# Second pair's B and C loaded in 2,048-byte pieces and turned by TensorE, first pair's loads first on two queues, seven filler matmuls

## The chip, the cores and the metric

The kernel runs on one core of a Trainium2 chip. The metric is the device time of one execution in microseconds (us); lower is better. A core has TensorE (PE; its weight loads are listed as PEld), VectorE (DVE), ScalarE (ACT), GpSimd (POOL) and SyncE (SP), each with an instruction queue of its own that is worked off in order. SP, and in the change ACT too, issue DMAs; all of them share 16 DMA engines. TensorE writes to PSUM banks, the other engines read those.

## What is computed

Two stages, cut to what matters here. The first is a scan over 768 positions for 4 x 8 (batch, head) pairs, in chunks; the second is a gated feed-forward layer on its result.

```python
# x: (4, 8, 768, 32), a: (4, 8, 768), B and C: (4, 8, 768, 16), all f32
cum = np.cumsum(log(clip(a, 1e-6, 1)) of the chunk)
L = np.exp(cum_i - cum_j), causal
y_intra = ((C @ B.T) * L) @ x
y_inter = (C @ state) * exp(cum)
y = y_intra + y_inter
state = exp(sum) * state + sum_j B_j x_j exp(cum_end - cum_j)
...
xf = y as (4 * 768, 256)
gate = 1 / (1 + np.exp(-(xf @ w_gate)))          # w_gate, w_val: (256, 1536)
out = (gate * (xf @ w_val)) @ w_out              # w_out: (1536, 256)
```

## The kernel before

The 768 positions are cut into six chunks of 128 (two halves of 64, the inner step of the scan). A *unit* is one chunk of one batch element with its eight heads; two units make a pair. For the first chunk (class `FirstUnit`) the pairs are laid out otherwise: unit u = 2 * late + k holds the *half* `late` of the chunk, and each half of the 128 partitions is another batch element. So the first pair (units 0 and 1, late = 0) is the first 64 positions of all four batch elements, and the second pair (units 2 and 3, late = 1) the other 64. Only the second pair needs a state from before it.

For a unit of the first chunk the steps are:

- `load_first`: SP loads B, C (tiles `bn`, `cn`) and x (`xn`) of a pair, two DMAs for each (line 274). For B and C the innermost contiguous run is 16 numbers, 64 bytes; for x it is 32 numbers, 128 bytes.
- `spread` (line 572): TensorE spreads the decays `apart` over partitions into `pa` (line 580), DVE scans them (line 586) into `ab`.
- `products` (line 377): TensorE transposes B and C (lines 386, 387) into `pt`, ACT copies the result to `bct`, B once and C masked for two groups (lines 397 to 401), and TensorE multiplies the two in `multiply` (line 464) into `pcb`.
- `decayed` (line 425): B times the decay at the end (`bd`, line 429, on DVE or POOL).
- `first_results` (line 604): DVE weighs the products by the decays (`weigh`, line 478, result `m`), TensorE multiplies by x (`within`, lines 490 and 497). The second pair adds the part from the state (line 624).
- `first_outputs` (line 629): ACT copies the output to `xw` (line 636); `first_states` makes the state from the rest.

The feed-forward layer takes the 1,536 hidden columns in 12 blocks f of 128. A weight tile holds two blocks of one matrix, so tiles w0 (gate) and w1 (value) serve blocks 0 and 1, w2 and w3 serve blocks 2 and 3, and so on to w11; w12 to w17 are `w_out`. Each is loaded with one DMA of 512 KB (lines 304 and 308, in runs of 2,048 and 1,024 bytes) and converted by `split_w` (DVE line 318, ACT 323, DVE 325, ACT 329, POOL 331); some are then cut into a high and a low part (`part_w`, lines 346 and 348). In the first chunk, blocks 0 to 5 use the converted weights as they are: blocks 0 to 3 in two halves, `half_gate` and `half_value` (line 714, 256 columns; half i takes the units of pair i), blocks 4 and 5 whole (line 804). From block 6 on, and in all later chunks, high and low parts are multiplied in three combinations (line 813). `proj` multiplies by `w_out` (lines 839, 850, 851) and stores the result.

TensorE starts with `WARM = 3` matmuls on zeros (line 126).

The order of the instructions in the engines' queues is set when the program is built, by a planner (`run`, line 180). Every piece of work is a task, a generator that yields steps; a step names its engine, an estimated cost, the keys it needs and the keys it makes. The planner keeps an estimated time for each engine, takes the step that could begin first, and among those of the same engine that could begin within `HOLD` of it the one with the earliest due time. `DUES` overrides the due times of single tasks; the load order at the start comes from `FIRST` with due times from -100 on. What the planner estimates sets only the order; on the chip, semaphores make an instruction wait for what it needs. SP issues all loads and stores in its planned order.

PSUM has three banks of the tag `mm` (used in turn by `pa`, the gates and values, `po`), one bank `py` (`warm`, `pt`) and four banks `pcb`.

Of the kernel before, what the change touches and what calls it, by code (L numbers as in the profile page):

```python
# [17 lines left out]
DUES = {  # L18
# [13 lines left out]
}  # L32
WARM = 3


FIRST = "b0 c0 w0 x0 w1 b1 c1 w2 x1 w3 r w4 w5 w6 w7 w8 w9"
LANES = 8
# [22 lines left out]
STATE = 30.0  # L60
SPARE = 1.0


# [4 lines left out]
def tile_ssd_then_gated_ffn(  # L68
# [111 lines left out]
    def run():  # L180

        free = {"sp": 1.0, "pe": 1.2 + 1.7 * WARM, "act": 3.5, "dve": 6.0, "pool": 6.2, "none": 0.0}
        port_free = [0.0]
        dma_free = 0.0
        landed = [0.0] * LANES

        turns, turn_of = [0.0] * 3, {}
        made = {}
        spare = {"y": [0.0], "banks": [0.0] * 3, "cb": [0.0], "g": [0.0] * 3, "o": [0.0] * 2}
        tasks.sort(key=lambda t: t[:2])  # L190
        while tasks:
# [78 lines left out]

    def load_first(tag, src, late, n):
        t = pair_of(tag, 0, 2 * late, n)
        for i in range(2):
            nc.sync.dma_start(  # L274
                t[i * L2 : (i + 1) * L2].rearrange("p u h n -> p (u h) n"),
                src[late * L2 : (late + 1) * L2, 2 * i * H : 2 * (i + 1) * H],
            )

    def load_a(c, b):
# [89 lines left out]
    class Unit:  # L369
# [7 lines left out]
        def products(self):  # L377

            c, b, u = self.c, self.b, self.u
            needs = [("bc", u)] if c else [("bc", u), ("b0", u // 2)]  # L380
            if c:
                needs += [("bct", u - 1 if c > 1 else -1), ("cb", u - 4), ("cd", u - 4)]
            yield step("pe", 0.24 if c else 0.45, needs, [("tp", u)], y=1)
            bn, cn = (got[k, c, b // 2][:, b % 2].rearrange("p h n -> p (h n)") for k in ("bn", "cn"))
            pt = ps_y.tile([P, 512], F32, tag="py", name=f"pt{self.nm}")
            nc.tensor.transpose(pt[:, :L], bn, eye)  # L386
            nc.tensor.transpose(pt[:, L : 2 * L], cn, eye)
            yield step("act", 0.9 if c else 1.1, [], [("bct", u)], y=-1)
            if c:
                self.bct = wk.tile([P, 4, L], F32, tag="bct", name=f"bct{self.nm}", bufs=4)  # L390
            else:

                if ("bct", b // 2) not in got:
                    got["bct", b // 2] = hp.tile([P, 2, 4, L], F32, tag=f"h{5 + b // 2}", name=f"bct{self.nm}")
                self.bct = got["bct", b // 2][:, b % 2]
            if u > 1:
                nc.scalar.copy(self.bct[:, :2].rearrange("p k l -> p (k l)"), pt[:, : 2 * L])
            else:
                nc.scalar.copy(self.bct[:, 0], pt[:, :L])
# [3 lines left out]
            if c == 0:  # L403
                yield step("pe", 0.47, [("cb", u - 1)] if u % 2 else [], [("cb", u)], **({} if u % 2 else {"cb": 1}))
                if u % 2 == 0:
                    got["pcb"] = ps_cb.tile([P, NQ, 512], F32, tag="pcb", name=f"pcb{self.nm}")
                multiply(got["pcb"], u % 2, self)
            elif u == NB + 1:
# [160 lines left out]
    class FirstUnit(Unit):  # L569


        def spread(self):

            u = self.u
            yield step("pe", 1.0, [("a0",)], banks=1)
            pa = ps_mm.tile([P, 512], F32, tag="mm", name=f"pa{u}")
            rows = slice(32 * (u // 2), 32 * (u // 2) + 32)
            for i in range(2):
                b = 2 * i + u % 2
                nc.tensor.matmul(  # L580
                    pa[i * L2 : (i + 1) * L2], of_b2[rows, b : b + 1].broadcast_to([32, L2]),
                    apart[rows].rearrange("p h l -> p (h l)"), start=True, stop=True,
                )
            yield step("dve", 1.22, [], [("scan", u)], banks=-1)
            self.dec = ld.tile([P, H, L2], F32, tag="ab", name=f"ab{self.nm}", bufs=NDEC)
            nc.vector.tensor_tensor_scan(
                out=self.dec.rearrange("p h l -> p (h l)"), data0=pa, data1=delta.rearrange("p h l -> p (h l)"),
                initial=0.0, op0=ALU.mult, op1=ALU.add,
            )
# [11 lines left out]
        def decays(self):  # L601
            yield from self.decayed()

    def first_results(*two):
# [24 lines left out]
    def first_outputs(late):  # L629

        for i in range(2):
            yield step("act", ACT_HALF, [("inter" if late else "y", 2 * late + 1)], [("xf", late)] if i else [])
# [3 lines left out]
            nc.scalar.copy(out, got["py", late][:, i, :, 0])  # L636

# [307 lines left out]
    def initial():  # L945
# [6 lines left out]
        yield step("none", 0.0, [], made)  # L952
        yield step("none", 4.9, [], [("a0",)])

    task(-60.0, "", initial())
# [7 lines left out]
    for late in range(2):  # L963
        for tag, src, n, needs, makes in (
            ("b", b4, N, [], [("b0", late)]),
            ("c", c4, N, [], [("bc", 2 * late), ("bc", 2 * late + 1)]),
            ("x", x4, D, [], [("xn", 2 * late), ("xn", 2 * late + 1)]),
        ):
            loads[f"{tag}{late}"] = load(
                2, 1.9 if tag == "x" else 1.5, needs, makes, lambda a=(f"{tag}n", src, late, n): load_first(*a)  # L970
            )
    for i in range(NW):
# [8 lines left out]
    def unit(due, c, b):  # L981
# [9 lines left out]
        if c or b > 1:  # L991
            task(due, f"before{u.nm}", u.before())
        task(due - (0.0 if c else 30.0), f"products{u.nm}", u.products())
        task(due, f"decays{u.nm}", u.decays())
        if c == 0 and b % 2:
            task(due, f"result{u.nm}", first_results(pair.pop(), u))
            task(due, f"outputs{u.nm}", first_outputs(b // 2))
# [71 lines left out]
```

## Time and profile before

| | us |
|---|---|
| median of 3 runs | 373.65 (373.58 to 373.71) |
| profiled execution | 374.85, its span 373.0 |
| TensorE busy in the span | 360.9 |
| mean granted TensorE clock | 0.982 of full |
| HBM read / written | 22.41 MB / 3.34 MB |

The span runs from the first to the last instruction that the profile records; the time of a run holds a little more. A line of the order of time has the start, the time taken, the engine, the line of the kernel, the operation, what it writes and reads, how many such instructions, and, in brackets, how long the engine had been idle before and what ended that. A matmul on f32 data appears as two PE instructions. "issue" means that the profile shows nothing that the engine waited for.

### The profile page before, as it was taken

Reading aid. Unit: us, or ns where it says so; the run is one execution under the profiler, and the core shown is the slowest. Engines: PE = TensorE matmul, PEld = TensorE weight load, DVE = VectorE, ACT = ScalarE, POOL = GpSimd, SP = SyncE. Lnnn points to the kernel's source line nnn. Section 1 sums busy time; section 2 is a strip of 40 time slices with the busy share of each in tenths; the row PEclk is TensorE's granted clock in tenths of the full one; section 3 lists DMA queues with packets and bytes.
Section 4 is the critical chain, followed back from the end, with each engine's and each line's share of the span. In section 5 each row is a group of like instructions: output and inputs, shape, how many; then the busy total and the mean of one; then the engine's idle time right before and its main releaser. Section 6 shows DMA issues by size and latency. Waiting matters only on the chain.

```text
span 373.0 us, 8123 instructions
## 1 busy us (share of the span) xinstructions
PE 360.9 (97%) x3376; PEld 287.0 (77%) x3376; DVE 157.0 (42%) x277; ACT 151.1 (41%) x314; POOL 150.1 (40%) x159
## 2 busy tenths in 40 slices
PE   7788999999999999999999999999999999999996
PEld 2267668877878888888878888788877788888885
DVE  4756557768435444553354622430224440222201
ACT  2656686423575411544511245430254420254400
POOL 4425476463797520244440045430144420145410
PEclk9669999999999999999999999999999999999999
DMA  6999996527236322502332300400000000000000
GB/s 121 208 233 184 243 314 169 96 44 122 67 30 113 30 71 60 106 22 34 26 99 82 89 4 6 53 10 29 30 1 2 2 2 28 30 0 0 2 28 28
DMA packets 89270, 26.27 MB, mean 70 GB/s; under 512 B 76306, under 2 KB 82002, under 8 KB 89234
## 3 DMA queue, kind: packets, MB, share of 16 engines
q1 hardware_dynamic: 89234, 25.76, 31.8%
q8 instruction: 26, 0.43, 0.5%
q14 instruction: 10, 0.08, 0.1%
HBM read 22.41 MB, written 3.34 MB: 69 GB/s over the span
## 4 chain that ended last, share of the span: by engine, by line
PE 88%; SPq 5%; DMA 4%; POOL 1%; issue 1%; DVE 0%; ACT 0%
PE pv L813 25%; PE pg L813 24%; PE po L850 15%; PE po L851 7%; PE po L839 6%; DMA cn<-in_C_dram 2%; SPq L304 2%; PE pcb L464 2%; PE pcb L490 2%; PE pcb L541 2%; SPq L262 1%; DMA bn<-in_B_dram 1%; SPq L274 1%; PE pcb L497 1%; POOL wr L331 1%; PE pt L386 1%
## 5 line engine op out<-in xcount | busy, mean ns | idle before, releaser
L781 POOL TENSOR_TENSOR h<-g,h 128x512 fp32r<-128x512 f32 x60 | 78.5, 1308 | 126.6 <-ACT h L779 126.3
L813 PE MATMUL pv<-xh,w 128*128 128x512 f32 x264 | 93.9, 396 | 0.0
L813 PE MATMUL pg<-xh,w 128*128 128x512 f32 x264 | 93.3, 394 | 0.0
L850 PE MATMUL po<-w,h 128*128 128x512 f32 x228 | 82.1, 402 | 0.0
L775 DVE TENSOR_TENSOR g<-pv,g 128x512 f32<-128x512 f32 x60 | 41.5, 691 | 93.0 <-PE pv L813 87.5
L779 ACT CAST h<-g 128x512 fp32r<-128x512 f32 x59 | 36.6, 621 | 75.7 <-DVE g L775 75.7
L851 PE MATMUL po<-w,h 128*128 128x256 f32 x228 | 63.9, 280 | 0.0
L813 PEld LDWEIGHTS pg<-xh,w 128*128 128x128 f32 x264 | 49.6, 188 | 10.8 <-issue 0.2
L813 PEld LDWEIGHTS pv<-xh,w 128*128 128x128 f32 x264 | 49.6, 188 | 10.7 <-issue 0.3
L813 PE MATMUL pv<-xl,w 128*128 128x512 f32 x132 | 51.5, 390 | 0.0
L813 PE MATMUL pg<-xl,w 128*128 128x512 f32 x132 | 51.4, 390 | 0.0
L850 PEld LDWEIGHTS po<-w,h 128*128 128x128 f32 x228 | 42.8, 188 | 11.0 <-issue 0.5
L754 ACT ACTIVATE g<-pg 128x512 f32<-128x512 f32 x68 | 40.7, 599 | 14.7 <-PE pg L813 13.8
L851 PEld LDWEIGHTS po<-w,h 128*128 128x128 f32 x228 | 43.0, 189 | 0.2
L866 ACT COPY o<-po 128x256 f32<-128x256 f32 x20 | 7.5, 373 | 65.7 <-PE po L851 65.1
L419 DVE TENSOR_TENSOR_SCAN ab<-ab,delta 128x512 f32<-128x512 f32 x20 | 28.0, 1406 | 8.3 <-DMA ab<-a_z 8.2
L868 DVE TENSOR_TENSOR o<-po,o 128x256 f32<-128x256 f32 x20 | 8.4, 424 | 49.6 <-ACT o L866 49.5
L813 PEld LDWEIGHTS pg<-xl,w 128*128 128x128 f32 x132 | 24.8, 188 | 4.8
L813 PEld LDWEIGHTS pv<-xl,w 128*128 128x128 f32 x132 | 24.8, 188 | 4.6
L348 POOL TENSOR_TENSOR w<-wr,w 128x512 fp32r<-128x512 f32 x18 | 23.8, 1326 | 9.7 <-ACT w L346 8.8
L331 POOL TENSOR_TENSOR wr<-wr 128x512 int32<-128x512 int32 x18 | 19.6, 1091 | 20.0 <-ACT wr L329 17.9
L839 PE MATMUL po<-wr,h 128*128 128x256 f32 x96 | 23.4, 393 | 0.0
(96 smaller groups left out, 371.1 us busy)
## 6 DMA issues: line engine op xcount, KB each, us to landing
ab<-a_z SPq DMA_DIRECT2D x40, 128.0 KB
wr<-in_moe_w_val_dram SPq DMA_DIRECT2D x6, 512.0 KB
wr<-in_moe_w_gate_dram SPq DMA_DIRECT2D x6, 512.0 KB
wr<-in_moe_w_out_dram SPq DMA_DIRECT2D x6, 512.0 KB
out_dram<-o SPq DMA_DIRECT2D x24, 128.0 KB
xn<-in_x_dram SPq DMA_DIRECT2D x10, 256.0 KB
bn<-in_B_dram SPq DMA_DIRECT2D x10, 128.0 KB
cn<-in_C_dram SPq DMA_DIRECT2D x10, 128.0 KB
```

What stands on the lines that cost most here:

```text
L331: nc.gpsimd.tensor_tensor(out=lw.bitcast(I32), in0=hw.bitcast(I32), in1=lw.bitcast(I32), op=ALU.add)
L348: engines[eng].tensor_tensor(out=lo, in0=lw, in1=hi.bitcast(F32), op=ALU.subtract)
L419: nc.vector.tensor_tensor_scan(out=t.rearrange("p h l -> p (h l)"), data0=t.rearrange("p h l -> p (h l)"), data1=delta.rearrange("p h l -> ...
L754: nc.scalar.activation(gs[k, f], pm, AF.Sigmoid)
L775: nc.vector.tensor_tensor(out=g, in0=pm, in1=g, op=ALU.mult)
L779: copies[eng](hh, g)
L781: engines[eng].tensor_tensor(out=hl, in0=g, in1=hh.bitcast(F32), op=ALU.subtract)
L813: nc.tensor.matmul(pm, w[:, part, kt, fs], xx[:, kt], start=(i == 0), stop=(i == 3 * NK - 1))
L839: nc.tensor.matmul(acc[:, :DM], hs[k, f][:, js], whole[NF + f // 2][:, f % 2], start=start, stop=stop, skip_group_check=True,)
L850: nc.tensor.matmul(acc, hh, w.rearrange("p i m -> p (i m)"), start=start, stop=False, skip_group_check=True)
L851: nc.tensor.matmul(acc[:, :DM], hl, w[:, 0, :], start=False, stop=stop, skip_group_check=True)
L868: nc.vector.tensor_tensor(out=o, in0=acc[:, DM:], in1=o, op=ALU.add)
```

## The change

- The first pair's C is issued from ACT's queue, ahead of ACT's first activation. B, the first weight, x and the second pair's B and C follow on SP in a new order.
- `load_rows` loads the second pair's B and C, for each one DMA of 64 pieces of 2,048 bytes: a partition holds 32 consecutive positions of one (batch, head), 16 numbers each (`rows`, 64 partitions).
- `turned` brings them into the layout of `bn` and `cn`: for each of the 16 columns and four 32-partition groups of the output one TensorE matmul, 64 rows of `rows` against 16 columns of the identity; 64 for B, 64 for C. ACT or DVE copies the PSUM bank.
- `first_pair` handles both units of a pair in one step where `products` handled one: four transposes into one bank, three ACT instructions over both units, then `multiply` for each.
- `warm_up` puts filler matmuls (identity times identity, f32, 128 columns) ahead of steps named in `FILLS`: four before the first pair's transposes, three before its first `multiply`. They write a bank `mm` that is not read.
- The second pair's `spread` steps need the first pair's products ("cb", 1) and, for the scan, its weighing ("mult", 1).
- The second of the `first_outputs` copies may go to DVE.
- The planner's starting times are other ones, and `DUES` is replaced as a whole.

```diff
 DUES = {
-    "ap": -250.3, "b0": -747, "c0": -1659.1, "w0": -247.3, "w1": -1093.4, "b1": -246.9, "c1": -287.9, "w2": -84.4,
-    "x1": -70.9, "w3": -405, "r": -84, "w7": -58.6, "w8": -58, "w9": -24, "w12": 14, "w13": 14, "w14": 5.5, "w15":
...
+    "clip": -453.5, "turned": -160, "w4": -92.4, "w7": -31.2, "w8": -27, "w9": -26, "w10": -4.4, "w11": -3.5, "w12":
+    -32.7, "w15": 17, "w16": -23.4, "w17": -29.2, "products0": -180, "xparts": 86, "spread0": -188, "decays0_0":
+    -184, "spread1": -187, "decays0_1": -183, "products0_1": -186, "result0_1": -182, "outputs0_1": -181,
+    "state0_1": -179, "spread2": -150, "before0_2": -171, "decays0_2": -172, "spread3": -149, "before0_3": -171,
+    "decays0_3": -172, "products0_3": -174, "result0_3": -170, "outputs0_3": -169, "state0_3": 20, "x1_0": -165.4,
...
-FIRST = "b0 c0 w0 x0 w1 b1 c1 w2 x1 w3 r w4 w5 w6 w7 w8 w9"
+FIRST = "b0 w0 x0 rows w1 x1 w2 w3 r w4 w5 w6 w7 w8 w9"
...
+FILLS = {"products0_1": {0: 4, 1: 3}}
+TURN = 1.2
...
-        free = {"sp": 1.0, "pe": 1.2 + 1.7 * WARM, "act": 3.5, "dve": 6.0, "pool": 6.2, "none": 0.0}
+        free = {"sp": 1.0, "pe": 0.6 + 1.7 * WARM, "act": 4.0, "dve": 5.4, "pool": 6.3, "none": 0.0}
...
+        def warm_up(many):
+
+            if many:
+                fill = ps_mm.tile([P, 512], F32, tag="mm", name="fill")
+            for _ in range(many):
+                nc.tensor.matmul(fill[:, :P], eye, eye, start=True, stop=True)
...
+            if eng == "pe" and tasks[n][5] in FILLS:
+                name = tasks[n][5]
+                nth[name] = nth.get(name, -1) + 1
+                warm_up(FILLS[name].get(nth[name], 0))
...
+    def load_rows():
+
+        got["rows"] = hp.tile([P, 2, 32, N], F32, tag="s0", name="rows")
+        for j, src in enumerate((Bm, Cm)):
+            nc.sync.dma_start(
+                got["rows"][: 2 * NB * H, j].rearrange("p t n -> p (t n)"),
+                src[:, :, L2:L].rearrange("b h (q t) n -> (b h) q (t n)", q=2),
+            )
+
+    def turned():
+
+        for j, tag in enumerate(("bn", "cn")):
+            yield step("pe", TURN, [("rows", 0)], banks=1)
+            pn = ps_mm.tile([P, 512], F32, tag="mm", name=f"pn{tag}")
+            rows = got["rows"][: 2 * NB * H, j]
+            for n in range(N):
+                for i in range(2):
+                    for q in range(2):
+                        p = i * L2 + q * 32
+                        nc.tensor.matmul(
+                            pn[p : p + 32, n * 16 : n * 16 + 16], rows[:, :, n],
+                            eye[: 2 * NB * H, : 2 * NB * H].rearrange("p (b q) -> p q b", q=2)[:, q, 16 * i : 16 * i + 16],
+                            start=True, stop=True, skip_group_check=True,
+                        )
+            eng = yield step(
+                ("act", "dve"), (0.4, DVE_HALF), [], [("bc", 2), ("bc", 3)] if j else [("b0", 1)], banks=-1
+            )
+            out = pair_of(tag, 0, 2, N).rearrange("p u h n -> p n (u h)")
+            copies[eng](out, pn[:, : 2 * P].rearrange("p (n b) -> p n b", b=16))
...
-            yield step("pe", 1.0, [("a0",)], banks=1)
+            yield step("pe", 1.0, [("cb", 1)] if u > 1 else [("a0",)], banks=1)
...
-            yield step("dve", 1.22, [], [("scan", u)], banks=-1)
+            yield step("dve", 1.22, [("mult", 1)] if u > 1 else [], [("scan", u)], banks=-1)
...
+    def first_pair(*two):
+
+        us, late = [t.u for t in two], two[0].u // 2
+        yield step("pe", 0.8, [k for u in us for k in (("bc", u), ("b0", late))], [("tp", u) for u in us], y=1)
+        pt = ps_y.tile([P, 512], F32, tag="py", name=f"pt0_{late}")
+        for k in range(2):
+            for j, tag in enumerate(("bn", "cn")):
+                at = (2 * k + j) * L
+                nc.tensor.transpose(pt[:, at : at + L], got[tag, 0, late][:, k].rearrange("p h n -> p (h n)"), eye)
+        yield step("act", 1.5 if late else 1.15, [], [("bct", u) for u in us], y=-1)
+        bct = hp.tile([P, 2, 4, L], F32, tag=f"h{5 + late}", name=f"bct0_{late}")
+        from_pt = pt.rearrange("p (u k l) -> p u k l", u=2, k=2)
+        many = 2 if late else 1
+        nc.scalar.copy(bct[:, :, :many], from_pt[:, :, :many])
+        for g in range(NG):
+            nc.scalar.mul(bct[:, :, 2 + g], from_pt[:, :, 1], of_g[:, g : g + 1])
...
+        for k, (t, u) in enumerate(zip(two, us)):
+            yield step("pe", 0.3, [], [("cb", u)], **({} if k else {"cb": 1}))
+            if k == 0:
+                pcb = ps_cb.tile([P, NQ, 512], F32, tag="pcb", name=f"pcb0_{late}")
+            multiply(pcb, k, t)
...
+    load_first("cn", c4, 0, N, nc.scalar)
     nc.scalar.activation(table, table, AF.Sigmoid)
...
+    loads["b0"] = load(2, 1.5, [], [("b0", 0)], lambda: load_first("bn", b4, 0, N))
+    loads["rows"] = load(2, 0.6, [], [("rows", 0)], load_rows)
+    task(-9.5, "turned", turned())
```

`rows` takes the tag `s0` of `hp`, a buffer that a weight's parts use later.

More of the change, by code (lines that the diff above doesn't have):

```diff
@@ L379, in products @@
             c, b, u = self.c, self.b, self.u
[L380 to L383, printed above, removed]
+            needs = [("bc", u), ("bct", u - 1 if c > 1 else -1), ("cb", u - 4), ("cd", u - 4)]
+            yield step("pe", 0.24, needs, [("tp", u)], y=1)
             bn, cn = (got[k, c, b // 2][:, b % 2].rearrange("p h n -> p (h n)") for k in ("bn", "cn"))
@@ L387, in products @@
             nc.tensor.transpose(pt[:, L : 2 * L], cn, eye)
[L388 to L399, printed above, removed]
+            yield step("act", 0.9, [], [("bct", u)], y=-1)
+            self.bct = wk.tile([P, 4, L], F32, tag="bct", name=f"bct{self.nm}", bufs=4)
+            nc.scalar.copy(self.bct[:, :2].rearrange("p k l -> p (k l)"), pt[:, : 2 * L])
             for g in range(NG):
@@ L602, in decays @@
             yield from self.decayed()
+    def first_pair(*two):
[13 more added lines that the diff above has]
+            nc.scalar.mul(bct[:, :, 2 + g], from_pt[:, :, 1], of_g[:, g : g + 1])
+        for k, t in enumerate(two):
+            t.bct = bct[:, k]
+            units[t.u] = t
+        for k, (t, u) in enumerate(zip(two, us)):
[3 more added lines that the diff above has]
+            multiply(pcb, k, t)
     def first_results(*two):
@@ L635, in first_outputs @@
             out = xw[0].rearrange("p k (i u s l) -> p k i u s l", i=2, u=2, s=2)[:, :, i, :, late]
-            nc.scalar.copy(out, got["py", late][:, i, :, 0])
+            copies[eng](out, got["py", late][:, i, :, 0])
     def first_states(late):
@@ L953, in initial @@
         yield step("none", 4.9, [], [("a0",)])
+        yield step("none", 0.3, [], [("bc", 0), ("bc", 1)])
     task(-60.0, "", initial())
@@ L963, in tile_ssd_then_gated_ffn @@
     for late in range(2):
[L964 to L971, printed above, removed]
+        makes = [("xn", 2 * late), ("xn", 2 * late + 1)]
+        loads[f"x{late}"] = load(2, 1.9, [], makes, lambda late=late: load_first("xn", x4, late, D))
+    loads["b0"] = load(2, 1.5, [], [("b0", 0)], lambda: load_first("bn", b4, 0, N))
+    loads["rows"] = load(2, 0.6, [], [("rows", 0)], load_rows)
+    task(-9.5, "turned", turned())
     for i in range(NW):
@@ L992, in unit @@
             task(due, f"before{u.nm}", u.before())
-        task(due - (0.0 if c else 30.0), f"products{u.nm}", u.products())
+        if c:
+            task(due, f"products{u.nm}", u.products())
         task(due, f"decays{u.nm}", u.decays())
         if c == 0 and b % 2:
+            task(due - 30.0, f"products{u.nm}", first_pair(pair[-1], u))
             task(due, f"result{u.nm}", first_results(pair.pop(), u))
```

21 lines of the change are left out of this document (10 added, 11 removed), and 21 rows, old and new, of the table DUES.

## Prediction

> **What bounds the kernel now.** I read first the page's busy shares and slices, then the busy time by stage, then the order of time in the first 50 us. From the page:
>
> ```profile
> span 373.0 us, 8123 instructions
> PE 360.9 (97%) x3376; PEld 287.0 (77%) x3376; DVE 157.0 (42%) x277; ACT 151.1 (41%) x314; POOL 150.1 (40%) x159
> PEclk9669999999999999999999999999999999999999
> ```
>
> TensorE is busy for 97% of the span; the rest runs beside it. So an edit can gain only TensorE's idle time and the time in which its clock is low, and pays for whatever work it puts on TensorE. The busy time of PE, PEld, DVE, ACT and POOL, cut where the stages change (each as busy time and instructions; the last three columns are the granted clock, the DMA share and GB/s):
>
> ```profile
> 0.00:11.46 11.46, 8.84 (x40) 3.46 (x40) 5.69 (x16) 3.76 (x8) 5.33 (x14) 1.00 0.74 131
> 11.46:21.18 9.72, 5.61 (x121) 2.63 (x121) 5.79 (x11) 5.69 (x15) 4.60 (x8) 0.50 0.97 262
> 21.18:25.12 3.94, 3.94 (x38) 2.69 (x39) 2.20 (x5) 1.62 (x3) 0.84 (x1) 0.50 1.14 203
> 25.12:50.53 25.41, 23.30 (x241) 16.73 (x240) 14.27 (x32) 18.23 (x40) 12.73 (x15) 1.00 0.92 216
> 50.53:94.60 44.07, 44.07 (x469) 35.48 (x462) 32.34 (x48) 20.59 (x42) 26.62 (x29) 1.00 0.59 137
> 94.60:362.00 267.40, 267.40 (x2435) 219.51 (x2434) 95.19 (x165) 100.46 (x205) 99.98 (x96) 1.00 0.18 35
> 362.00:373.03 11.03, 7.74 (x45) 6.54 (x43) 1.46 (x4) 0.75 (x2) 0.00 (x0) 1.00 0.10 37
> ```
>
> From 50.53 to 362 nothing is idle. The change does not touch the tail. What can be won lies ahead of 50.53: 2.62 us idle in the first row (1.09 of it before the first warm-up matmul, which stays: 1.53), 4.11 in the second, 2.11 in the fourth, 7.75 together; and half a clock over 5.61 + 3.94 = 9.55 us of busy time. Two finer windows place the clock: 0.73 in the twelfth microsecond is 0.54 us at half, a fall at 11.46, and 0.94 is 0.12 us at half, a rise at 25.12.
>
> ```profile
> 3.00:4.00 1.00, 1.00 (x3) 0.48 (x2) 0.00 (x0) 0.00 (x0) 0.04 (x1) 1.00 0.88 97
> 10.00:11.00 1.00, 1.00 (x20) 0.50 (x20) 0.79 (x1) 0.98 (x3) 0.21 (x1) 1.00 1.22 115
> 11.00:12.00 1.00, 1.00 (x8) 0.49 (x6) 1.00 (x1) 0.00 (x0) 0.83 (x1) 0.73 0.64 77
> 20.00:21.00 1.00, 0.00 (x0) 0.00 (x0) 0.49 (x2) 0.44 (x2) 0.10 (x1) 0.50 1.01 387
> 25.00:26.00 1.00, 1.00 (x6) 0.91 (x5) 0.71 (x3) 0.08 (x1) 0.32 (x1) 0.94 0.41 51
> ```
>
> Who makes TensorE wait there, in order of time:
>
> ```profile
> 1.51 1.38 SPq L274 DMA_DIRECT2D cn<-in_C_dram  x2
> 4.30 0.22 DVE L889 TENSOR_SCALAR ac<-a 64x128 f32<-64x128 f32 x1 [2.04 <-DMA a<-in_a_dram]
> 5.61 1.78 PE L580 MATMUL pa<-apart,of_b 32*64 32x512 f32 x8
> 7.61 0.43 DVE L318 TENSOR_SCALAR wr<-wr 128x512 f32<-128x512 f32 x1 [2.25 <-DMA wr<-in_moe_w_val_dram]
> 8.15 1.18 DVE L586 TENSOR_TENSOR_SCAN ab<-pa,delta 128x512 f32<-128x512 f32 x1
> 8.91 0.30 PE L386 MATMUL pt<-eye,bn 128*128 128x128 f32 x1 [1.52 <-DMA bn<-in_B_dram]
> 10.79 1.04 POOL L331 TENSOR_TENSOR wr<-wr 128x512 int32<-128x512 int32 x1 [0.86 <-ACT wr L329]
> ...
> 15.85 0.45 PE L386 MATMUL pt<-eye,bn 128*128 128x128 f32 x1 [1.58 <-DMA bn<-in_B_dram]
> 16.36 0.69 DVE L478 TENSOR_TENSOR m<-pcb,ab 128x512 f32<-128x512 f32 x1
> 16.55 0.37 ACT L397 COPY bct<-pt 128x256 f32<-128x256 f32 x1 [0.69 <-PE pt L387]
> 20.71 0.37 ACT L636 COPY xw<-pcb 128x256 f32<-128x256 f32 x1 [0.56 <-DVE m L505]
> 21.18 2.05 PE L714 MATMUL pg<-xw,wr 128*128 128x256 f32 x4 [1.44 <-issue]
> ```
>
> The first pair waits for its B until 8.91 and the second for its own until 15.85. The first pair is weighed only at 16.36, behind the second pair's scan on DVE, and its output is copied at 20.71. So the first gate, the start of the dense work, waits until 21.18.
>
> **The change, part by part.** *Loads.* Today B and C of a pair are two DMAs of 64 KB each in 64-byte runs, and the window at 10 us shows such traffic at 115 GB/s against 387 for the weights in 2,048-byte runs at 20 us. The second pair's 256 KB then cost 2.3 us of the queue; as 2,048-byte pieces 0.7. That 1.6 us moves the weights forward; by itself it buys nothing at the end, where TensorE rules, and it is inside the idle terms. Two of the first pair's issues go to ACT (0.69 us each by the row at 1.51), ahead of ACT's first use at about 8 us: nothing, or 1.38 if an early weight wanted ACT. They share the queues with a, which lands at 4.30 today; between 0 and 1.2 us later (two 64 KB pieces at 115 GB/s). I take 0.3, which hides: TensorE warms until 5.68 and the first pair's weighing waits for its products, not its scans. First pair's B and C are together 256 KB, 2.3 us at that rate. The queue carries its first 97 GB/s in the window at 3 us, so they are in between 5.3 and today's 8.9; I take 6.3, a microsecond for a's packets beside them and for landing.
>
> *First pair first.* Spreads end at 7.4 (row at 5.61), four fillers at 8.3, transposes 8.8, three ACT instructions of 256 columns at 0.37 to 9.9, products 0.69 to 10.7, two weighings of 0.69 to 12.1, then the pair's own products and one copy of 0.37: 13.2. The first weight needs its conversion: today's first took 7.61 to 11.83, 4.2 us; landed at about 7.6, but with DVE held by two scans of 1.2 and two weighings, it ends at 14.2 to 14.5. With the turn's share on TensorE I put the first gate at 15, six microseconds ahead of today's.
>
> *The turn.* For B and for C 64 small f32 multiplications, two instructions each: 256, with as many weight loads. The trace has nothing of just this shape (64 rows, 32 columns, 16 streamed). The nearest:
>
> ```profile
> 23.16 1.16 PE L464 MATMUL pcb<-bct 32*64 32x128 f32 x32
> 27.45 0.45 PE L490 MATMUL pcb<-m,xn 64*32 64x64 f32 x32
> 28.57 0.69 PE L624 MATMUL pcb<-cd,m 32*64 32x64 f32 x32
> 49.91 0.69 PE L464 MATMUL pcb<-bct 32*64 32x128 f32 x32
> ```
>
> From 27.45 to 28.57 run the 96 instructions of a pair (lines 490 and 497) with the same 64-row, 32-column weights: 11.7 ns each, 3.0 us for 256. Line 464 as a whole takes 22 ns each at full clock (5.5 us) and 36 at half (9.3). Below, 0.45 us for 32 less the 0.22 of one is 7.4 ns (1.9 us). I take 3.0, the row with the same weights. The Trainium skill, page TensorE: Matmul & The Clock Gate, section Wait — 56ns, not 53.3ns?, says that start-to-start never drops below about 25 ns however few columns are streamed; that would make it 6.4 us, an estimate from the page; the 11.7 ns of the row above disagrees, with neighbours in other parts of the array.
>
> The two copies behind the turn (0.37 each on ACT, or DVE's) delay only the second pair. That pair's spreads now wait for the first pair's products and weighing: TensorE's 1.8 us of them moves behind, the scans behind them too, and the second pair's weighing waits for these. The gates of the first half cover it: the eight half-width groups of four that need only the first pair's output, 0.86 each by the starts at 33.67 and 34.53 below, 6.9 us. Without that cover the second pair's chain would add its length to the idle time; that is in the bound there.
>
> *Fillers.* (Rows below.) Seven f32 products of 128 columns. The full-width group of line 804 takes 1.72 us (46.15 to 47.87) for four instructions of 512 columns, 0.43 each; 128 columns are 0.11, two instructions a filler: 1.5 us for seven. From nothing (all inside waits) to 3.0 (half clock); I count 1.5.
>
> ```profile
> 33.67 1.03 PE L714 MATMUL pv<-xw,wr 128*128 128x256 f32 x4
> 34.53 1.03 PE L714 MATMUL pg<-xw,wr 128*128 128x256 f32 x4
> ...
> 46.15 1.89 PE L804 MATMUL pg<-xw,wr 128*128 128x512 f32 x4
> 47.87 0.27 PE L386 MATMUL pt<-eye,bn 128*128 128x128 f32 x1
> 50.53 0.50 PE L813 MATMUL pg<-xh,w 128*128 128x512 f32 x1
> ```
>
> *Clock.* If it holds, the 9.55 us of half-clock work shrink; streams by 2 (2.05 us against 1.03 for a half-width group), small products by 1.7 (1.16 against 0.69): I take 4.2, between nothing and 4.8.
>
> *Due times.* They reorder the whole program. x of the second chunk goes up in SP's queue, waits there for the first pair's results, and holds the weights queued behind it for its 256 KB: between 0.7 us (387 GB/s) and 2.3 (115, 64-byte runs); its runs are 128 bytes, and I take 1.4. From 50.53 on there is no idle time to win; a loss is bounded in the rivals.
>
> *Sum.* Given back: idle 7.75 and clock 4.2, 11.95 us. Added on TensorE: turn 3.0 and fillers 1.5. What becomes late next is the conversion of the second to fourth weight (over 3 us apiece through DVE, ACT and POOL, held by 1.4 on SP) and ACT's 1.1 us between transposes and products, of which the fillers cover 0.6: I take 2.5 us of new idle, near a third of the old 7.75, because the second pair's work is there to fill it; the bounds are 0 and 7.75. Net 11.95 - 4.5 - 2.5 = 4.95 us. The profiled execution took 374.85 with a span of 373.0; the median of the runs shown is 373.65, 0.65 over the span. So the span becomes about 368.1 and the time **368.7 us**; the first gate on split weights, hidden block 6 (50.53 today), starts at about 45.6.
>
> **Rivals.**
>
> 1. *The clock falls all the same.* It fell at 11.46 though PE was busy 8.84 of 11.46 us and its longest gap was the 1.52 at 8.91; what had run just before was small tiles. The fillers are 0.9 us ahead of the transposes and 0.6 behind. The Trainium skill, same page, section What's actually happening, has the clock drop after an idle window of about 3.4 us and rise after a busy one; this trace shows a fall without any such gap, so it disagrees, and holding gaps short proves nothing. A half clock from 11.46 until the gates have run some 3 us takes back about half of the 4.2 us: 370.8.
>
> 2. *Weights come late.* Gates from 15 on use up a converted weight every 1.7 us (two groups of 0.86), and a conversion takes DVE, ACT and POOL in turn. ACT is already at 18.23 of 25.41 us between 25.12 and 50.53. If new idle is 5 instead of 2.5: 371.2.
>
> 3. *The turn at line 464's pace*, 22 ns: 5.5 us, 371.2. This is the side on which the page's floor of 25 ns lies; that alone would give 372.1.
>
> 4. *The second chunk is not earlier.* Its last low part is written shortly before its first gate:
>
> ```profile
> 91.86 0.42 DVE L561 TENSOR_TENSOR xl<-pcb,xh 128x256 fp32r<-128x256 f32 x1 [0.44 <-ACT xh L555]
> 94.20 0.59 PE L813 MATMUL pg<-xh,w 128*128 128x512 f32 x1
> ```
>
> It ends at 92.28 and the gate starts at 94.20: with that chain unmoved only 1.9 us are gained, 371.75. Against it: the loads ahead of the chain go early with the rest, and DVE has 12 us free in that stage.
>
> 5. *Slower: the turn stalls TensorE at half clock*, 36 ns each (the row at 23.16), 9.3 us, 6.3 over my term, with its tiny tiles keeping the clock low, 2 more: 4.95 - 6.3 - 2.1 = 3.4 us lost, 377.1. It turns from gain to loss where the turn takes over 8 us, 31 ns each. For it: all its weights lie on the same 64 rows, so fewer neighbours overlap than in the row at 27.45. Against it: full-array loads hide under the stream everywhere after 50 us.
>
> **How the numbers follow.** Forecast 0.50; clock 0.18; weights 0.10; turn at 22 ns 0.07; second chunk 0.06; slower 0.06; and 0.03 that losses just meet gains. The low end is no new idle and the turn at 1.9 us: 11.95 - 3.4 = 8.5 us, 365.1; I stop at 365.6, since some wait for ACT remains. The high end takes in rivals 1 to 4: 372.0. About 0.2% (0.75 us) is what a measurement can tell from no change; on that scale slower 0.08 (rival 5, and 0.02 of rival 4 with a longer wait), same 0.06 (the 0.03, and as much of rivals 2 and 4), faster the rest, 0.86.
>
> **What would show it.** Right: the transposes of the first pair at 8 to 9, the first line-714 gate near 15, the first gate on split weights near 45.6, PEclk without the two 6s, the turn in 3 us. Wrong: PE idle over 4 us between 15 and 45; PEclk still 0.5 past 18; turn instructions over 20 ns apart; idle PE in the slices after 50 us, where today there is none.

## The result: slower by 3%, and the profile after

The changed kernel takes 384.77 us (median of 4 runs, 384.41 to 386.36) against 373.68 us (373.58 to 374.74); the ratio is 1.0297, interval 1.0273 to 1.032. The forecast was 368.7. One execution among those reported below, of 1235 us, took over three times as long as all others of its kernel and is left out. The profiled execution took 386.36 us. Its page, the same rows as were shown of before, and one row of the DMA queues:

```profile
span 384.6 us, 8663 instructions
...
PE 368.3 (96%) x3646; PEld 293.6 (76%) x3646; DVE 157.8 (41%) x276; ACT 151.3 (39%) x311; POOL 152.7 (40%) x159
...
PEclk9758899999999999999999999999999999999999
...
q8 instruction: 28, 0.46, 0.5%
```

TensorE's busy time grew by 7.4 us (368.3 less 360.9) and its idle time by 4.2 (16.3 less 12.1): together the 11.6 us of the span. The low clock has not gone, it has moved. Busy time by stage shows where (cut where the clock changes and at the first gate on split weights, 60.14; columns as before):

```profile
0.00:14.76 14.76, 13.00 (x198) 7.34 (x198) 6.62 (x17) 4.63 (x9) 6.07 (x15) 1.00 0.87 141
14.76:31.83 17.07, 9.33 (x239) 6.54 (x238) 6.01 (x10) 4.83 (x11) 2.63 (x4) 0.50 0.94 276
31.83:42.07 10.24, 6.93 (x176) 4.74 (x174) 4.58 (x13) 3.70 (x9) 3.26 (x7) 1.00 0.96 279
42.07:45.48 3.41, 3.20 (x8) 2.58 (x9) 1.36 (x4) 2.68 (x7) 1.10 (x2) 0.50 1.20 136
45.48:60.14 14.66, 14.66 (x56) 10.31 (x55) 9.13 (x18) 9.89 (x21) 10.84 (x10) 1.00 0.67 156
60.14:384.60 324.46, 321.22 (x2976) 262.11 (x2974) 130.12 (x217) 125.61 (x259) 128.76 (x124) 1.00 0.21 43
```

Up to that gate the kernel needs 60.14 us where it needed 50.53; from there to the end 324.46 where it needed 322.5. So 9.6 of the 11.6 us are lost ahead of 60.14. The idle time there is 13.0 us (1.76, 7.74, 3.31 and 0.21) against 8.84 before. The view of waits says what ended it (us in total, times, longest):

```profile
PE pncn L315 <- issue: 5.9, 1, 5.9
PE pcb L680 <- issue: 3.2, 1, 3.2
PE pcb L521 <- issue: 1.8, 1, 1.8
```

Three waits make 10.95 us, and "issue" means that the profile shows no engine, no buffer and no transfer of data that was waited for. The order of time shows that each of them cuts through a group of equal instructions whose inputs were all there:

```profile
11.86 2.20 PE L315 MATMUL pnbn<-eye,rows 64*32 64x16 f32 x128 [0.49 <-DMA rows<-in_B_dram]
...
15.17 0.64 PE L521 MATMUL pcb<-m,xn 64*32 64x64 f32 x23
...
17.61 0.33 PE L521 MATMUL pcb<-m,xn 64*32 64x64 f32 x5 [1.79 <-issue]
...
18.68 1.02 PE L315 MATMUL pncn<-eye,rows 64*32 64x16 f32 x52
...
25.65 1.38 PE L315 MATMUL pncn<-eye,rows 64*32 64x16 f32 x74 [5.95 <-issue]
...
29.76 1.91 PE L773 MATMUL pg<-xw,wr 128*128 128x256 f32 x4
...
40.57 0.33 PE L680 MATMUL pcb<-cd,m 32*64 32x64 f32 x4 [3.21 <-issue]
...
60.14 0.79 PE L872 MATMUL pg<-xh,w 128*128 128x512 f32 x1
```

The turn of C stops after 54 of 128 matmuls (2 more run ahead of the row of 52) and TensorE stands for 5.95 us. I counted all of TensorE's instructions in the trace from the first one, matmuls, weight loads and the 54 semaphore instructions: the three waits stand ahead of the 450th, the 706th and the 1218th, which are 256 and twice 256 apart. The page has 2 x 3646 matmuls and weight loads and 28 transfers on queue 8, "instruction", of 16 KB each (0.46 MB by 28): 260 instructions a transfer. So TensorE's own instructions come in blocks of 256, by the same DMA engines as the data, and at these three places, I conclude, the next block had not come. The traces of all kernels reported here bear it out: of their 19 "issue" waits on TensorE (over 0.15 us), 15 stand ahead of the 450th, the 706th or the 1218th instruction, whatever that instruction is, and the other 4 ahead of a first gate. The DMA queues (packets, MB, share of the 16 engines) from 17.7 to 23 us, and from 23 to 24.2 us:

```profile
q1 hardware_dynamic: 890, 1.73, 98.0%
```

```profile
q1 hardware_dynamic: 232, 0.44, 100.0%
q8 instruction: 1, 0.02, 5.6%
```

While TensorE stands, from 19.7 to 23, the queue of the data has the DMA engines to 98%, and no block moves. Then one does (it starts at 23.03 and takes 1.08 us), and the turn goes on at 25.65. **The turn's 512 instructions, 256 matmuls and 256 weight loads, are as many as two whole blocks, used up in 4.6 us of work, while the block that TensorE had run out of began to move only 7.5 us after TensorE came to the position one block earlier:** it came there at 15.5, stood, and went on from there at 17.61, 5.4 us before the block moved.

Before has such a wait too, of 1.50 us inside one group of line 714, where no data is waited for either, and it stands ahead of the 706th instruction:

```profile
33.12 0.71 PE L714 MATMUL pg<-xw,wr 128*128 128x256 f32 x2 [1.50 <-issue]
```

I had taken it for idle time to be won.

### The profile page after: what moved, and what is told of

The parts are those of the page before. It is cut to its first block, busy times and chain, and to the rows that moved or that the text cites. A ratio compares the mean times of both kernels' runs of the same rounds, so it can differ in the third digit from the quotient of the medians.

```text
span 384.6 us, 8663 instructions
## 1 busy us (share of the span) xinstructions
PE 368.3 (96%) x3646; PEld 293.6 (76%) x3646; DVE 157.8 (41%) x276; ACT 151.3 (39%) x311; POOL 152.7 (40%) x159
## 4 chain that ended last, share of the span: by engine, by line
PE 93%; issue 3%; DMA 2%; SPq 1%; ACT 0%; DVE 0%
PE pv L872 24%; PE pg L872 24%; PE po L909 14%; PE po L910 7%; PE po L898 6%; PE pcb L521 2%; PE pg L773 2%; PE pv L773 2%; PE pcb L495 2%; PE pcb L572 2%; DMA rows<-in_B_dram 2%; PE pcb L528 1%; PE pv L863 1%; PE pg L863 1%; PE pa L611 1%
## 5 line engine op out<-in xcount | busy, mean ns | idle before, releaser
L909 PEld LDWEIGHTS po<-w,h 128*128 128x128 f32 x228 | 42.8, 188 | 10.9 <-issue 0.2
L378 POOL TENSOR_TENSOR wr<-wr 128x512 int32<-128x512 int32 x18 | 20.6, 1150 | 28.4 <-ACT wr L376 23.3
L450 DVE TENSOR_TENSOR_SCAN ab<-ab,delta 128x512 f32<-128x512 f32 x20 | 25.0, 1265 | 2.4 <-DMA ab<-a_z 2.4
```

What stands on the lines that cost most here:

```text
L378: nc.gpsimd.tensor_tensor(out=lw.bitcast(I32), in0=hw.bitcast(I32), in1=lw.bitcast(I32), op=ALU.add)
L450: nc.vector.tensor_tensor_scan(out=t.rearrange("p h l -> p (h l)"), data0=t.rearrange("p h l -> p (h l)"), data1=delta.rearrange("p h l -> ...
L909: nc.tensor.matmul(acc, hh, w.rearrange("p i m -> p (i m)"), start=start, stop=False, skip_group_check=True)
```

## The experiments

The theory, **instruction supply**: time is lost because many short instructions in a row use up the blocks faster than a full DMA queue brings them. The rivals: the **turn's work** itself or its tiles at a low clock (my rival 5); the **transfers and the order**, which make weights late (my rival 2). Every time is a median with the lowest and highest run; a ratio is to before's runs on the same chip.

### The same turn in few instructions, and before with many

The first edit takes the turn's instructions away and leaves its transfers, copies and order; its matmuls are 4 wide ones for each tensor, and the second pair's B and C are not turned:

```
-            for n in range(N):
...
-                        nc.tensor.matmul(
-                            pn[p : p + 32, n * 16 : n * 16 + 16], rows[:, :, n],
...
+                    nc.tensor.matmul(
+                        pn[p : p + 32, : 2 * P], rows[:, :, 0], flat[:, : 2 * P],
```

> The changed kernel with the turn's 64 small matmuls a tensor replaced by four wide ones (256 columns each): about the same time on TensorE, 16 instructions with their weight loads in place of 256 for each of B and C. The second pair's B and C are then not turned. Refill theory (TensorE's instructions come in blocks by DMA, and the turn uses up two blocks faster than they arrive while the data queue is full): the waits of 1.8 and 5.9 us in the middle of a stream of matmuls go, and the time falls to 367 to 373 us. Order theory (the new due times and load order are what costs): the order is the same, so it stays above 381. Turn theory (TensorE's time for it): stays above 381 too.

374.11 us (371.92 to 377.37), ratio 0.9998 [0.9968, 1.0029]. Its largest waits:

```profile
PE pg L772 <- DVE ab L616: 1.8, 1, 1.8
PE pcb L494 <- DVE m L508: 1.1, 1, 1.1
```

No issue wait is left among them, and 10.7 us are gone. The median lies 1.1 us above the range of the supply theory and 7 us below what the rivals asked for. The 4 wide matmuls stream as many columns (1024 for a tensor) and take 1.3 us for both.

The second edit adds the cost to before, and nothing else of the change: 128 matmuls of the turn's shape ahead of the first pair's products, on data that is there long before.

```
+        if not late:
...
+                for n in range(N):
+                    for p in range(0, P, 32):
+                        nc.tensor.matmul(
+                            more[p : p + 32, n * 16 : n * 16 + 16], eye[:L2, 2 * n : 2 * n + 32], eye[:L2, :16],
```

> The kernel before, in its own order and with its own loads, with 128 small f32 matmuls of the turn's shape (their result is not used) ahead of the first pair's products with x. Refill theory: one or two waits of over 1.5 us that no semaphore explains appear within or soon behind them, at a block's end, and the time rises by 4 to 9 us, to 378 to 383. Order and turn theories: only TensorE's own time for them, at most 4 us and partly in idle time, so 374 to 377.

386.22 us (383.96 to 386.77), ratio 1.03 [1.0258, 1.0343]. The waits, and the added instructions in the order of time:

```profile
PE more L620 <- issue: 5.1, 1, 5.1
PE pcb L490 <- issue: 4.1, 1, 4.1
PE pg L723 <- issue: 3.1, 2, 1.7
```

```profile
17.78 2.32 PE L620 MATMUL more<-eye 64*32 64x16 f32 x157
25.19 1.42 PE L620 MATMUL more<-eye 64*32 64x16 f32 x92 [5.08 <-issue]
```

The turn's instructions alone make before as slow as the changed kernel, though they run for only 3.7 us (2.32 and 1.42). The price is above what every theory expected; the supply theory had its kind and place right, and was too low because one lack of instructions is followed by the next. The waits of 5.08 and 4.10 us and the longer one on line 723, 1.68, stand ahead of the 450th, the 706th and the 1218th instruction; the other on line 723, 1.44, is that of the first gate, which before has too. The clock is at half for 27.3 us, against 13.7 of before.

### The transfers kept away from it

The weights from the fifth on and the second chunk's B, C and x wait for the second pair's transposes:

```
-        loads[f"w{i}"] = load(1, 1.35, [], [("raw", i)], lambda i=i: load_w(i))
+        loads[f"w{i}"] = load(1, 1.35, [("bct", 3)] if i > 3 else [], [("raw", i)], lambda i=i: load_w(i))
```

> The changed kernel with the weights from the fifth on, and the second chunk's B, C and x, loaded only when the second pair's B and C have been multiplied out (SP waits for them), so that the DMA queue is nearly empty while TensorE needs its blocks; the turn is as in the change. Refill theory with the data queue as its cause: a block's transfer starts within 2 us of the request in place of 4 to 7, the waits up to 30 us shrink from 7.7 us to under 3 together, and the first gate comes before 24 us (29.8); the time falls below 380 although weights come later. If a block takes this long whatever else is queued: the waits stay above 6 us and the time is 384 or more.

386.04 us (384.92 to 387.39), ratio 1.0308 [1.0269, 1.0348]: the time was missed, and the first gate comes at 25.76, not ahead of 24.

```profile
PE pcb L680 <- issue: 2.8, 1, 2.8
PE pt L431 <- ACT bct L437: 1.9, 1, 1.9
PE pncn L315 <- issue: 1.8, 1, 1.8
...
PE pcb L521 <- issue: 0.7, 1, 0.7
```

The two waits ahead of 30 us shrink from 7.7 to 2.5 us, as they must if the full queue holds the blocks back; they do not go. What is won there is lost behind: the held loads lead to a second chunk that waits for ACT, and the clock falls twice more, at 38 and at 73 us. It supports the full queue as the cause of the delay; it is no remedy.

### The second pair without a turn, in short runs

```
-FIRST = "b0 w0 x0 rows w1 x1 w2 w3 r w4 w5 w6 w7 w8 w9"
+FIRST = "b0 w0 x0 b1 c1 w1 x1 w2 w3 r w4 w5 w6 w7 w8 w9"
```

> The changed kernel with the second pair's B and C loaded as before, in 64-byte runs, and no turn; the first pair first, two queues, fillers and due times as in the change. Refill theory: no wait inside a stream before 25 us, the first gate at 15 to 18 us, 366 to 371 us in all, faster than the kernel before. Order theory: above 380, since all of the order but the turn is kept.

379.68 us (379.29 to 380.2), ratio 1.0138 [1.0108, 1.0168]. Neither theory's time was met (366 to 371, or above 380). The first gate starts at 15.20, just where I had put it, and it does not help:

```profile
PE pg L773 <- POOL wr L378: 3.3, 1, 3.3
PE pv L773 <- issue: 3.0, 1, 3.0
PE pcb L521 <- DVE m L509: 2.0, 1, 2.0
PE pv L872 <- POOL w L395: 1.6, 1, 1.6
```

With the turn gone, weights are waited for (3.3 and 1.6 us behind POOL) and another block is late (the 3.0 us stand ahead of the 706th instruction). So rival 2 is real too: a first gate at 15 is ahead of the weights.

### A turn on VectorE

Pieces of B and C are interleaved in one tile, and one VectorE instruction turns blocks of 32 by 32; TensorE's 512 instructions go. A second kernel leaves the fillers out as well (`FILLS = {}`), a third has before's table of due times.

```
+        to = got["rows"][:, 0].rearrange("(i k j) t n -> i j k (t n)", i=2, j=2)
...
+            for i in range(2):
+                nc.sync.dma_start(to[i, j], of[i])
...
+                nc.vector.transpose(at, rows[:, 0].rearrange("p t n -> p n t"))
```

> The order of the kernel after, its pieces of 2048 bytes and its 7 fillers; only the turn goes from TensorE to one VectorE instruction that transposes blocks of 32 by 32 (B and C interleaved in one tile, 4 loads in place of 2), so that 512 instructions leave TensorE's stream and B and C are still turned. Theory (the instruction blocks that ran out cost the 10.95 us of issue waits): the waits go as they did with the few wide matmuls, and the 1.3 us of those matmuls go too: 372 to 374.5 us, no issue wait of over 1 us before block 6. Rival (the pieces themselves, their transfer or the order cost it): 378 us or more with the first gate behind 20 us.

> As the VectorE turn, without the 7 fillers (2.1 us of TensorE in the kernel after). If the fillers hold the clock up over a window as I forecast, the clock falls a window (3.4 us) or more earlier, near 12 to 15 us, and the time is 0.5 to 3 us above that of the run with the fillers. If they only take time, 0.5 to 2 us below it.

> The VectorE turn with the table of due times of the kernel before (its 2048-byte pieces, new FIRST and fillers stay). If the new table is worth something on its own: 1 to 4 us above the run with it. If the order matters little once the blocks are not used up: within 1 us of it. What it tells: whether the order, rather than the turn, is what can beat the kernel before.

379.86 us (378.14 to 380.17), 378.08 without fillers (377.53 to 378.45) and 384.98 with the old table (384.81 to 385.24). The first expectation was missed by 5 us, in the main for a reason of its own:

```profile
PE pcb L514 <- DVE m L502: 7.3, 1, 7.3
PE pcb L673 <- issue: 2.7, 1, 2.7
...
17.68 1.03 DVE L312 STREAM_TRANSPOSE rows<-rows 128x512 f32<-128x512 f32 x1 [5.30 <-DMA rows<-in_C_dram]
```

The four loads, which write every second partition, land 5.8 us later than the two of the changed kernel, and VectorE stands in front of them with the first pair's weighing behind it. The expectation "no issue wait of over 1 us before block 6" was missed as well: 2.7 us stand ahead of the 706th instruction, so blocks can be late without the turn. This kernel says little on the theory. What the pairs say: the version with fillers is 1.8 us slower, but its profiled run has that wait of 2.7 us and the one without has none, so this is not the price of the fillers alone. The new order is worth 5 us over the old table, where 1 to 4 were expected. The old table's profiled run has an issue wait of 6.5 us, and that one is no missing block: it stands ahead of the first gate, the 348th instruction, and ends as ACT finishes the output copies (21.49 to 22.16), which ACT had behind its copy of the turned B, held until 21.05 by VectorE's turn.

### A turn on TensorE in 64 instructions

Pieces of 4096 bytes, 32 rows for each tensor; 16 transposes of 32 rows by 64 columns turn a tensor, and two copies spread it. That is the turn of the changed kernel in 64 instructions for 512. With the fillers, and without:

```
-                    for q in range(2):
...
+                nc.tensor.matmul(
+                    pn[:L2, n * 32 : n * 32 + 32], got["rows"][at, :, n],
+                    eye[at, at], is_transpose=True, start=True, stop=True, skip_group_check=True,
```

> The turn stays on TensorE, but as 16 transposes of 32 rows by 64 columns for each tensor (64 instructions of its stream in all, not 512) from pieces of 4096 bytes (32 rows of each tensor, one load for each); everything else as in the kernel after. The VectorE turn had failed for another reason: its four loads landed at 17.7 us in place of 11.86, and VectorE stood in front of them. Theory (the instruction blocks that ran out are the loss): issue waits before block 6 under 3 us in sum (10.95 in the kernel after), first gate before 20 us, 371 to 375 us. Rival (turning on TensorE or the new order loses by itself, whatever the number of instructions): 378 us or more without issue waits.

> The same without the 7 fillers (2.1 us of TensorE). If they hold the clock up over a window: the clock falls a window (3.4 us) or more earlier and the time is 0.5 to 3 us above the run with them. If they only take time, as the pair on VectorE's turn showed (378.08 against 379.86): 0.5 to 2 us below it.

> The turn of 32 transposes with the 7 fillers once more, for its trace: the first profile of it was taken in a disturbed run. Theory: the fillers hold the clock through the first gates (no fall before 24 us, 10 to 13 us later than without them), and still the time is 373 to 377 us, at or above the 373.2 us without them, since they add 2.1 us of TensorE ahead of the first gate and the fall comes later, under gates in place of waits. Rival (the fillers save clock time and something else takes it back): an idle of 2 us or more that the run without fillers does not have.

With the fillers 375.49 us (372.78 to 377.75), 0.5 above the range expected, ratio 1.0026 [0.9994, 1.0059], and in the second series, on another chip, 373.9 (372.84 to 378.21), 1.0013 [0.9979, 1.0048]. **Without them 373.20 us (372.01 to 373.61), ratio 0.9973 [0.9961, 0.9985]**: a version that beats both kernels, the one before by 0.27% with the whole interval below 1. Fewer instructions for the same turn give back 9.3 to 10.9 us of the changed kernel's 384.77, and issue waits are down to 0.4 us in the profiled run with fillers and 0.6 without. The fillers cost 2.3 us by the first series and 0.7 by the second. The stages of the version without fillers, and its turn:

```profile
0.00:11.20 11.20, 8.26 (x52) 3.34 (x52) 6.09 (x17) 4.01 (x8) 5.15 (x15) 1.00 0.89 141
11.20:19.84 8.64, 8.32 (x141) 4.83 (x141) 4.35 (x9) 4.94 (x9) 2.19 (x3) 0.50 1.06 285
19.84:23.00 3.16, 3.16 (x26) 2.28 (x25) 2.27 (x3) 2.16 (x5) 1.91 (x6) 0.74 1.03 367
23.00:45.92 22.92, 21.94 (x218) 15.82 (x219) 17.77 (x33) 15.80 (x33) 14.46 (x15) 1.00 0.99 260
45.92:370.20 324.28, 321.10 (x2976) 262.05 (x2974) 130.45 (x217) 125.77 (x259) 129.22 (x124) 1.00 0.23 47
```

```profile
11.52 1.08 PE L312 MATMUL pnbn<-eye,rows 32*64 32x32 f32 x16 [1.59 <-DMA rows<-in_B_dram]
...
15.99 1.11 PE L312 MATMUL pncn<-eye,rows 32*64 32x32 f32 x16
```

Its first gate on split weights starts at 45.92 (before 50.53). Idle time up to it is 4.24 us against 8.84, busy time 41.68 against 41.69: the turn's 2.2 us of work are balanced by less time at half clock (10.2 us against 13.7, by the trace's clock) and by work that has moved behind the gate. For 1.8 of the 4.6 us are lost again: from that gate to the end it takes 324.28, before 322.5. The busy time by line from that gate on, of before and of this version, says part of why:

```profile
L464 PE MATMUL pcb<-bct 32*64 32x128 f32 x296 | 6.5, 280 | 0.0
...
L386 PE MATMUL pt<-eye,bn 128*128 128x128 f32 x17 | 4.8, 285 | 0.0
L387 PE MATMUL pt<-eye,cn 128*128 128x128 f32 x17 | 4.6, 272 | 0.0
```

```profile
L493 PE MATMUL pcb<-bct 32*64 32x128 f32 x320 | 6.9, 280 | 0.0
L429 PE MATMUL pt<-eye,bn 128*128 128x128 f32 x19 | 5.4, 286 | 0.0
L430 PE MATMUL pt<-eye,cn 128*128 128x128 f32 x19 | 5.2, 272 | 0.0
```

Four transposes and 32 products of the second chunk, which before has ahead of the gate, now stand behind it (of before's 296 products, 8 started just ahead of the gate). By their starts that is about 1.1 us: 0.6 for the products, from 49.91 to 50.53 in before, and 0.1 for each transpose. The other 0.7 is open. The changed kernel's last stage has the same.

The fillers do reach the clock, in some runs: of the 17 runs with them 9 have a mean granted clock of 0.999 or more and take 372.78 to 374.71 us (median 373.14); the other 8 have 0.981 to 0.995 and take 375.49 to 378.21. The 9 runs without fillers all have 0.981 to 0.986, and take no longer than the former. In the profiled run with fillers (375.85 us) the clock falls at 14.5 us, 3.2 us later than without (11.3), and again at 35.0, within its largest wait, which ends at 35.37:

```profile
PE pv L771 <- DVE h L795: 2.5, 1, 2.5
```

So the expectation "no fall before 24 us" failed in that run, and that the fillers win nothing held. The wait of 2.5 us is also what the rival foretold, an idle of over 2 us that the run without fillers does not have; whether the other runs of over 375 us have it too, no trace shows.

### Two attempts to go on from there

`TURN = 0.55` in the plan, and `FIRST` with `rows` ahead of `x0`, both without fillers.

> The turn of 32 transposes without fillers, with the duration of the turn in the plan put from 1.2 to 0.55 us, so that the planner can order its neighbours for it. If the plan's order is what is left: 371 to 372.5 us. If the transfers set the order whatever the plan says: 373 us, as without it, within 0.5.

> The turn of 32 transposes without fillers, with the pieces of the second pair loaded ahead of the first pair's x in place of behind it. Its turn waited 1.6 us for the pieces at 11.5 us. If that wait is on the path: 371.5 to 372.5 us. If x is then late for the first pair's products, which follow the turn at 14.4 us: 373 to 375 us.

375.66 us (375.01 to 375.91), 1.005 [1.003, 1.0069], and 377.01 (376.17 to 379.58), 1.0085 [1.0047, 1.0123]: both worse than 373.2, and outside what was expected. Their waits are spread over many small ones of about a microsecond (behind transfers, ACT and DVE); I did not find one cause. The 0.55 us are no correct duration either: the transposes of a tensor took 1.08 and 1.11 us, at half clock, nearer to the 1.2 of the plan before.

## Why the prediction was wrong, step by step

- **The turn, 3.0 us: the step that failed.** I priced it as 256 matmuls by their spacing, and its rivals, 3 and 5, were other spacings. B's 128 matmul instructions took 2.20 us, 17 ns each at full clock, between my 11.7 and rival 3's 22. With C's 1.02 and 1.38 at half clock that is 4.6, 1.6 us over the term. What I left out is where the instructions come from: 9.45 us more waits for blocks (10.95 less before's 1.50). Rival 5 had the turn stall TensorE, by tile and clock at 36 ns; the place was right, the mechanism not. The Trainium skill, page TensorE: Matmul & The Clock Gate, section Wait — 56ns, not 53.3ns?, has starts no closer than 25 ns; the 17 ns here lie below if each instruction counts, and above (34 ns) if the two of an f32 product count as one. The Trainium skill, page Runtime: NRT & Kernel Launch, section Instruction fetch mechanics, says that instructions come in 16 KiB blocks of 256, and that crossing a block's end is mostly hidden. The size agrees with this trace; the hiding does not, with 5.95 us at one block's end.
- **Idle time, 7.75 given back and 2.5 new.** Net 5.25 less was forecast; the changed kernel has 4.2 more. The difference, 9.4 us, is as large as those 9.45. In the version with 64 instructions idle time falls by 4.6, near the forecast.
- **Clock, 4.2.** Wrong by all of it: up to the gate on split weights busy time grew by 5.4 us, the turn's 4.6 and the fillers' 2.1 less some 1.1 of work that moved behind that gate, which leaves some 0.2 for the clock. The fall at 14.76 comes 3.3 us later than before's but ahead of the first wait for a block (from 15.8): so far rival 1 was right. Half clock then lasts to 31.83 and comes back from 42.07 to 45.48, 20.5 us against before's 13.7; where the same fall meets no long wait for a block, in the profiled run of 64 instructions with fillers, it lasts 6.8 and 3.4 us. The 4.2 were also too much: a held clock is worth about the 2.1 us of the seven fillers that hold it, as held runs with them equal runs without (373.14 and 373.20), or 3.3 by the other runs of the same kernel (median 376.44). No kernel held it without fillers.
- **Fillers, 1.5:** 2.1 by their busy time.
- **First pair first:** transposes at 8.66, as forecast. The first gate, forecast at 15, came at 29.76, behind 7.7 us of waits for blocks and the half clock. Where it does come at 15.20 (the short runs), the weights are late, as rival 2 said.
- **"From 50.53 on there is no idle time to win":** true, but I let the gain up to there carry through to the end, and 1.8 to 2.0 us do not: 1.1 of it is work that before has ahead of that gate and the new order behind it. Even free of block waits the forecast of 368.7 was missed, by more than this: the version with block 6 at 45.92, beside the forecast 45.6, takes 373.20 (its profiled run 372.01).
- **Due times:** without old and new order in one kernel free of block waits their part stays open; on VectorE's turn the new order was 5 us better, where the old one had its first gate wait behind that turn's copies on ACT.

## What to carry to other kernels

Count the instructions of an edit, weight loads included, beside their duration: a run of several hundred short ones in the first tens of microseconds, while the data queue is full, cost more here in waiting for the stream than in work; do the same in fewer, wider ones. An "issue" wait in the middle of a group of equal instructions, at the same count of instructions in kernel after kernel, is the sign of it, and before's trace already had one; an "issue" wait at the start of a group can be something else, as the old table's was. And a gain ahead of a saturated stage counts only after the work that has moved into that stage is taken off.

## What the runs showed of the hardware that was not expected

- TensorE's instruction blocks (16 KB, 256 instructions) share the DMA engines with data. Counted by position in the stream, the changed kernel's second block started to move 7.5 us after TensorE came to the position one block before, with the data's queue at 98%; 2.3 us with the weights held back. In the three waits TensorE goes on 1.5 to 1.7 us after a block has moved. What asks for a block, and when, I infer from positions alone.
- From 10 to 20 us of VectorE's turn the DMA moves 112 GB/s at a share of 0.51, where the changed kernel has 256 GB/s at 0.96. Its four loads write every second partition, but 2104 of the 2523 packets there have under 512 bytes and belong to other loads; which of the two slows it stays open.
- Seven fillers hold the clock at full speed in 9 runs of 17, on one program. Stretches of one clock last 3.41 us or whole multiples of it (3.41, 10.24 and 17.07 in the changed kernel, 13.66 in before).
